# Polysketch attention and a multiplicative FFN on one core: 65 steps of the early program written in another order

## The chip, the cores and the metric

The kernel runs on one core of a Trainium2 chip. The core has five engines that each work through their own list of instructions in order: TensorE (PE in the profile; its weight loads are PEld), VectorE (DVE), ScalarE (ACT), GpSimd (POOL) and SyncE (SP, which here only issues DMAs). An instruction that waits for another engine holds up everything behind it on its own list. The metric is the device time of one execution in microseconds (us); before the change it is 245.37 us, the median of three runs.

## The reference

Sixteen heads (4 batches of 4) of sequence 1088 and width 32 go through an attention that sketches keys and queries, and the result, 4352 tokens of 128, goes through a feed-forward net whose two first products are multiplied element by element:

```
a = einsum('rd,bhsd->bhsr', S1, x);  b = einsum('rd,bhsd->bhsr', S2, x)     # r = 8
phi(x) = (a outer b), flattened to 64
kv  = einsum('bhsf,bhsd->bhfd', phi(k), v);   z = sum over s of phi(k)
att = einsum('bhsf,bhfd->bhsd', phi(q), kv) / (einsum('bhsf,bhf->bhs', phi(q), z) + 1e-6)
x   = att as (4352, 128)
out = (((x @ w1) * (x @ w2)) @ w3) @ w_out                                # 128 -> 1024 -> 1024 -> 128
```

The float64 words of the inputs are loaded raw and turned to float32 on the chip.

## The kernel before, in words

The kernel is one long straight program. `make_steps` defines 1,179 named steps, each a closure that issues one to a few dozen instructions; the string `ORDER` lists the names, and the kernel calls the steps in that order. Each instruction is tied to the one ahead of it on its engine, so `ORDER` is the order of every engine's list. Nothing is rescheduled later. `SLOTS` names the buffer that the n-th tile of a kind gets (for the kind `b` a PSUM bank), `POOL`, `ACTS` and `CPV` name steps that run on GpSimd, ScalarE or VectorE in place of their default engine.

Names of steps: `k0` to `k3` are the four batches of keys, `q0`, `q1`, ... parts of the queries, `w0` to `w10` the weights' conversions, `g0.4a` and the like the FFN of a group of 512 tokens (`a` the product with w1, `c` its copy out of PSUM, `b` the product with w2, `m` the multiplication of both), `s.` the sketch matrices, `warm` idle matmuls on zeros. The steps that matter for what follows:

- For each batch of keys, `k*.lead` and `k*.rest` split k into a coarse and a fine part (tile `kk`), `k*.gram0` to `gram4` multiply them on TensorE into the Gram matrix (`ps_g`, L659): nine columns of tokens, four heads, two products, each issued as two weight loads and two matmuls, 288 instructions in all.
- `k*.Gm`, `Gt`, `Ga`, `Gb` split that matrix on VectorE (`G_g`, `G_t`, `G_a`, `G_b`), `k*.T0` and `T1` multiply it with the sketches (`ps_T`, L883 to L891), `k*.Ta` and `Tb` split the result (`T_p`, L898 to L904), `k*.N0` and `N1` make the matrices for the denominator (`ps_N`, L912) and `k*.Na`, `Nb` split those (`N_g`, `RC`). `k0.kv0` to `kv3` accumulate the sketched keys with v (`ps_kv`, L769).
- `s.R` (L355) replicates the sketches to all heads, `s.c` copies them to `Sc`, `s.blkh` and `s.blk` make `Rh` and `RS` from it on GpSimd. `q0.A0` (L1038) needs `Rh`.
- `q0.C0t` is a VectorE transpose of `ps_c` (L1050), `q1.Ct` another one (L1130). `q0.xc0`, `xc1` (L1274) and `q0.xT0`, `xT1` (L1291) make `xT`, the input of the first FFN group, whose first product is `g0.4a` (L1799). `q1.pt0` and `q1.pt1` (L1246) transpose `ph` of the next queries, `q1.x` (L1297) multiplies it with `kz`.
- `k2.lead0` is VectorE work of 1152 columns that `k2.rest0` on GpSimd and then `k2.gram0` wait for; `k2.ab` (L727) sketches the keys of batch 2.

```
    for name in ORDER.split():
        n = len(traced)
        steps.pop(name)()
        ...
    for ins in traced[seen:]:
        if ins.engine in chained:
            if ins.engine in last:
                tc.add_manual_dep(ins, last[ins.engine].name, behind, reason="order")
            last[ins.engine] = ins
```

Of the kernel before, what the change touches and what calls it, by code (L numbers as in the profile page):

```python
# [26 lines left out]

SLOTS = {
    "b": 
        "012345670214657210671306537457462512346127340273014526045721472352140327540542370673245716"  # L30
        "210605643174306437107523543106572361507514502371054643535436051532410354273245554744570504"
        "7734023146507073701426351241254057163771361764573436046273673572571236574127105",
    "k_g": "0101",
# [48 lines left out]
kr1.load k2.zero k1.tr1 k1.kT1 kr0.kp warm9 k0.N0 warm10 k0.Na warm11 k0.T1 k0.kv0 k0.Tc k0.Tb k0.N1 k0.Nb k0.Nh q1.rm
q0.al k0.Nf q0.phi0 q0.phi1 q0.A1 q0.smy w1.m1 k1.max q0.sty q0.shy k0.kv3 k0.kv1 k0.kv2 q0.sly s.KS k0.kvr kr1.tr
k0.kvm w1.m0 kr1.kT q0.p01 q1.C0 q1.C1 q0.C1 k0.kzt k2.loadr q0.pt0 q0.C1t q0.scy q0.p2 k0.kz q0.pt1 k0.kvc kr1.ab
k0.kqt q0.p12 q0.dn q0.de q0.rc w1.j0 q0.pc0 q0.pc1 q0.x0 k1.kT0 q0.x1 q0.xs0 q0.xs1 q0.xt0 w1.a0 q1.A0 k2.load
w0.load k1.lead0 q0.xc0 q0.xc1 k0.kq w1.a1 k2.max q0.xt1 k1.ab q0.xT0 q0.xT1 g0.4a q1.load g0.5a q1.sm w0.m1 q1.st
# [5 lines left out]
g0.1m k2.gram1 k2.gram2 q3.max k2.gram3 g0.0c k2.kT0 k1.Nb q1.xT k2.gram4 q3.l2 k2.ab q2.A0 q2.C0 q2.C1 q3.l1 k1.kp0
v1.zero w9.c k2.abt g1.5a g1.5c g1.1a q2.Ct g1.7a q2.At q3.rm q3.A0 k0.Nr q2.sm q3.C0 q3.C1 k2.Gm v1.loadr q2.st w2.m
q2.sh g1.1c g1.2a k1.kp1 g0.6m q3.Ct g1.0a g1.7b k3.load v1.load g1.5b q3.At k2.Gt k3.loadr w2.c k2.Ga g0.0b w9.j
q2.sl g1.7c w6.c g1.6a k1.kv0 q3.sm k2.Gb w5.load q2.sc q2.al g1.0c k2.Gc g1.7m q2.p01 q3.st k1.kv2 k1.kv3 q3.sh w9.m
k1.kv1 k2.T0 k1.kvr q3.sl q2.p2 k2.T1 q2.p12 q2.dn q2.de g1.4a q2.rc k3.max g0.3b g0.0m g1.1b kh3.load g1.4c k2.Ta
g1.2b q3.sc g1.2c w5.c k2.Tc k1.kvc k1.kqt k1.kq g0.3m q3.p01 g1.6c g1.3a g1.5m g1.3b q2.bs q2.phi0 q2.pT0 g1.2m g1.3c
q2.x q2.load k2.N0 k2.Tb k3.lead0 w9.a1 k2.N1 g1.4b q3.al q3.p2 q3.p12 q2.xT0 g2.5a k3.kT1 g2.5c g2.6a q3.dn q3.de
k2.Na g1.3m g2.4a g2.3a w5.m g2.4b g2.6c k3.rest0 g1.0b k2.Nr q3.rc g1.1m g1.4m g1.6b k2.Nb g0.2b kr1.kp w6.j q4.tr
g2.4c g1.6m w7.load w7.c q3.bs q4.max q2.restT w6.m w5.j w2.j q4.l2 w3.load w9.a0 k3.gram0 k3.gram1 k3.gram2 q3.load  # L100
w7.j q3.phi0 k3.gram3 k3.gram4 g2.2a k3.Gc g2.1a g1.0m w2.a0 g2.6b g2.0a g2.4m g2.1c f6.t w6.a0 w4.load g2.3b w2.a1
g2.2b g2.2c g2.0c w6.a1 g2.1b q3.pT0 k3.Gm g0.2m k3.Gt k3.kT0 v3.load w7.m f6.m w5.a1 w5.a0 g2.3c k3.Ga k3.Gb g2.3m
w7.a0 g2.1m w3.m g2.6m q3.x k3.T0 k3.T1 f2.t w3.c w3.j w8.load g2.0b q3.xT0 g3.1a f6.o k3.Ta g3.0a g3.0b g2.7a g2.7b
q4.l1 w7.a1 q4.rm g3.0c g3.0m g2.5b v3.loadr g3.3a w4.c g2.0m g2.2m g3.1c g2.5m g2.7c g2.7m v2.zero g3.6a k3.Tb
v2.loadr k3.ab f4.t k3.Tc k3.abt w4.j g3.3c w3.a1 q4.A0 q4.C0 q4.C1 q4.At k3.N0 k3.N1 v2.load w3.a0 f0.t k2.kp1 f4.m
w4.m g3.6c q3.restT q6.tr g3.6b g3.6m q4.Ct q4.sm w10.load f0.m k2.kp0 f4.o g3.1b f0.o g3.1m qr.max q6.max k3.kp1
q4.st k2.kv0 w4.a1 k3.kp0 k2.kv3 k2.kv1 k2.kv2 k2.kvr q4.sh qr.l2 k3.kv0 k3.kv1 f3.t k2.kvc k3.kv3 k3.kv2 k3.Na w4.a0
qr.l1 qr.rm q4.sl q4.sc q4.al k3.kvr k3.kvc g3.4a q6.l2 g3.4c g3.4b q4.p01 k3.Nr g3.3b q6.l1 w8.c g3.5a k3.Nb g2.4o
g3.4m f1.t f3.m w10.c k3.kqt g3.5c w8.m g3.3m q4.p2 q6.rm k3.kq f1.m f1.o q6.A0 q6.C0 w10.j q6.C1 g3.1o f3.o w8.j
q4.p12 q6.At g3.2b w10.m q6.Ct q4.dn g3.7a q6.sm q6.st w8.a0 w10.a0 qr.A0 qr.C0 qr.C1 g3.0o g2.1o g3.7c w10.a1 g0.3o  # L110
qr.Ct qr.At q6.sh q4.de g1.4o q4.rc q4.bs g3.5b q4.na w8.a1 f2.m f2.o q6.sl q6.sc g2.3o f7.t qr.sm g3.5m q4.nb q4.nm
g3.2a qr.st g3.2c g1.6o q4.nr q4.ne q4.nn q4.phi0 g0.2o q6.al k2.kqt f5.t g3.2m f5.m f5.o q4.phi1 q4.pT0 g3.7b g3.7m
qr.sh g3.6o f7.m k2.kq g0.4o q4.pT1 f7.o v.s v.t q4.x q4.xT2 q6.p01 g3.4o q6.p2 g2.7o g1.2o q6.p12 qr.sl g0.6o q6.dn
q6.de g1.5o q4.xT0 qr.sc qr.al q6.rc q6.bs q4.xT1 q6.nb q6.na q6.nm q6.nr q6.ne v.1 q6.nn q6.phi0 q4.xT3 q6.phi1 o.S3
q6.pT0 h4.s1 q6.pT1 g0.1o g0.0o g0.5o g0.7o g1.0o h4.s2 g3.5o g0.oT g1.7o q6.x g1.1o g2.5o qr.p01 qr.p2 qr.p12 qr.dn
g3.3o qr.de qr.rc qr.bs qr.phi0 qr.pT0 g3.2o q6.xT0 q6.xT1 q6.xT2 o.S1 g2.2o v.2 g3.7o q6.xT3 qr.x qr.xT0 g1.3o g2.0o
# [33 lines left out]
def make_steps(ctx, tc, q, k, v, S1, S2, moe_w1, moe_w2, moe_w3, moe_w_out, out):  # L150
    nc = tc.nc
    dve, act, pe, pool, sp = nc.vector, nc.scalar, nc.tensor, nc.gpsimd, nc.sync
    B, H, S, D = q.shape
# [689 lines left out]
    def k_end(b):  # L843
        a = acc[b]
        tag = "t"

# [63 lines left out]
        def by_head(o, P, x, start, stop):  # L910
            for h in range(H):
                pe.matmul(o[h * D:(h + 1) * D], P, a["Tp"][:, x, h], start=start, stop=stop,  # L912
                          tile_position=(0, h * D), skip_group_check=True)
# [1021 lines left out]
```

## Time and profile before

| what | value |
|---|---|
| runs | 245.28 to 245.43 us, median 245.37 us |
| span of the profiled execution, first to last instruction | 244.1 us |
| what lies around the span (median less span; the profiled execution has no time of its own besides) | 1.27 us |
| TensorE clock granted, mean | 0.998 |
| busy: PE / DVE / ACT / POOL | 97% / 85% / 51% / 66% of the span |
| PE instructions shown | 2724 matmuls and 2724 weight loads |
| DMA | 22.06 MB, most of it in the first 100 us |
| instructions fetched by DMA during the span | queue q8: 21 transfers, 0.34 MB; queue q14: 10 transfers, 0.08 MB |

The share of busy time is a mean over stages. TensorE is counted busy for nearly the whole span, but in the first microseconds part of that is the idle matmuls on zeros. "issue" as the cause of a wait means that the engine waited for nothing that the profile shows.

### The profile page before, as it was taken

What the parts mean: (1) busy time and instruction counts of PE and PEld (TensorE: products, weight loads), DVE (VectorE), ACT (ScalarE), POOL (GpSimd) and SP (SyncE); (2) the same over time, 40 slices, a digit from 0 to 9 for tenths busy, and PEclk for the clock granted to TensorE, in tenths of its full rate; (3) what the DMA queues carried; (4) which work ended last, traced back from release to release, by engine and by line L of the source; (5) the groups of instructions that cost most, each with busy time, mean ns of one, the idle gap of its engine ahead of it and who ended that gap; (6) DMA issues with size and microseconds to landing.
All of it is one profiled execution on the core that took longest, in us unless ns stands there. A gap on an engine that the chain in (4) does not pass through costs nothing.

```text
span 244.1 us, 6745 instructions
## 1 busy us (share of the span) xinstructions
PE 236.2 (97%) x2724; PEld 129.8 (53%) x2724; DVE 206.7 (85%) x421; ACT 123.5 (51%) x246; POOL 161.9 (66%) x203
## 2 busy tenths in 40 slices
...
GB/s 201 265 143 325 181 227 190 6 197 224 220 141 251 188 217 190 59 1 3 3 0 0 4 0 3 59 113 3 1 0 0 0 3 0 0 1 3 12 90 93
DMA packets 31935, 22.06 MB, mean 90 GB/s; under 512 B 21280, under 2 KB 26528, under 8 KB 31904
## 3 DMA queue, kind: packets, MB, share of 16 engines
...
q8 instruction: 21, 0.34, 0.6%
...
q14 instruction: 10, 0.08, 0.1%
...
## 4 chain that ended last, share of the span: by engine, by line
PE 87%; DMA 5%; ACT 2%; POOL 2%; DVE 1%; issue 1%; POOLq 0%; SPq 0%
PE b_ps L1809 12%; PE ps_o L1835 12%; PE ps_X L1673 11%; PE a_ps L1799 11%; PE ps_o L1759 10%; PE ps_w3o L534 6%; PE ps_Y L1673 6%; PE ps_Z L1673 3%; PE ps_g L659 2%; PE ps_x L1527 2%; PE ps_ac L1374 2%; DMA qh<-in_q_dram 2%; DMA k<-in_k_dram 2%; PE ps_or L1824 2%; POOL ph L1208 1%; PE idle_ps L255 1%
## 5 line engine op out<-in xcount | busy, mean ns | idle before, releaser
L1673 PE MATMUL ps_X<-xd,wv 64*128 64x512 f32 x112 | 36.3, 593 | 0.0
L1799 PE MATMUL a_ps<-xT,w 128*128 128x512 f32 (+1 forms) x80 | 36.1, 562 | 0.0
L1809 PE MATMUL b_ps<-xT,w 128*128 128x512 f32 (+1 forms) x80 | 35.6, 555 | 0.0
L1804 ACT COPY ffa<-a_ps 128x512 f32<-128x512 f32 (+1 forms) x38 | 20.1, 540 | 29.2 <-PE a_ps L1799 26.7
L1707 POOL TENSOR_TENSOR hc<-hc 128x512 f32<-128x512 f32 x16 | 20.7, 1304 | 15.7 <-DVE hc L1685 15.5
L1835 PE MATMUL ps_o<-ab,w3o 128*128 128x512 f32 x64 | 29.6, 600 | 0.0
L1680 ACT COPY hc<-ps_X 128x512 f32<-128x512 f32 x38 | 21.3, 590 | 16.1 <-PE ps_X L1673 12.9
L1815 DVE TENSOR_TENSOR ab<-ffa,b_ps 128x512 f32<-128x512 f32 (+1 forms) x40 | 23.9, 623 | 4.9 <-PE b_ps L1809 4.1
L501 POOL TENSOR_TENSOR w3c<-w3c,cv_m 128x512 int32<-128x512 int32 x16 | 21.2, 1344 | 4.2 <-DVE w3c L495 4.1
L1673 PEld LDWEIGHTS ps_X<-xd,wv 64*128 64x128 f32 x112 | 14.9, 186 | 13.1 <-issue 10.9
L1799 PEld LDWEIGHTS a_ps<-xT,w 128*128 128x128 f32 x80 | 14.1, 189 | 13.9 <-issue 8.8
L1809 PEld LDWEIGHTS b_ps<-xT,w 128*128 128x128 f32 x80 | 14.4, 190 | 13.1 <-issue 8.1
L1673 PE MATMUL ps_Y<-xd,wv 64*128 64x512 f32 x48 | 19.7, 594 | 0.0
L1835 PEld LDWEIGHTS ps_o<-ab,w3o 128*128 128x128 f32 x64 | 11.6, 190 | 13.4 <-issue 13.0
L534 PEld LDWEIGHTS ps_w3o<-wo,w3T 128*128 128x128 f32 x128 | 15.3, 192 | 2.4 <-issue 2.4
L534 PE MATMUL ps_w3o<-wo,w3T 128*128 128x128 f32 x128 | 15.7, 276 | 0.0
L1759 PE MATMUL ps_o<-hc,w3o 128*64 128x512 f32 x32 | 15.1, 595 | 0.0
L1759 PE MATMUL ps_o<-tt,ws 128*64 128x512 f32 x32 | 13.7, 594 | 0.0
L1680 ACT COPY hc<-ps_Y 128x512 f32<-128x512 f32 x14 | 8.1, 592 | 9.7 <-PE ps_Y L1673 6.6
L263 ACT ACTIVATE cv_c<-raw 128x1024 f32<-128x1024 f32 (+1 forms) x13 | 13.0, 1014 | 0.0
L1540 ACT COPY xd<-ps_x 64x256 f32<-64x256 f32 x24 | 8.8, 367 | 7.2 <-PE ps_o L1835 6.8
...
## 6 DMA issues: line engine op xcount, KB each, us to landing
...
```

The costliest lines, as they stand in the source:

```text
L263: act.activation(dst, hi.bitcast(F32), ACT.Prelu, scale=2.0 ** -112, alpha=-2.0 ** 32)
L501: pool.tensor_tensor(d, d, x["m"][:, i * 512:(i + 1) * 512], ALU.add)
L534: pe.matmul(t["o"], w3T[ko][:, c], wo[:, c], start=c == 0, stop=c == NC - 1)
L1673: pe.matmul(x[bank], stat(j, u)[:, i * 128:(i + 1) * 128], rows(j, u), start=new, stop=True, tile_position=(u * 64, 0), skip_group_check=True)
L1680: cp(n(y))(x[k], x[bank])
L1707: on(f"h{g}.{i}m{k}").tensor_mul(both[0][k], both[0][k], both[1][k])
L1759: pe.matmul(acc_o[bank][half[0]:half[1]], w(i), x(i), start=n == 1, stop=n == (2 if j == 3 else 4), tile_position=(0, half[0]), skip_group ...
L1799: pe.matmul(x["a"][:, :w], w_of(0, c), xT[g][:, c0:c0 + w], start=True, stop=True)
L1804: cp(f"g{g}.{c}{su}c")(x["s"][:, :w], x["a"][:, :w])
L1809: pe.matmul(x["b"][:, :w], w_of(1, c), xT[g][:, c0:c0 + w], start=True, stop=True)
L1815: dve.tensor_mul(ab_sb[g, c][:, c0:c0 + w], x["s"][:, :w], x["b"][:, :w])
L1835: pe.matmul(o_ps[g], w3o[:, c], ab_sb[g, c], start=n == 1, stop=n == NC)
```

## The change

65 steps stand elsewhere in `ORDER`, all between the 30th and the 345th name. No step is added or removed, and none runs on another engine. (`CPV` loses three names of steps whose branch for batches 2 and 3 never asks `CPV`.) `SLOTS` is rewritten where the order in which tiles are made has changed, so that every tile shares its buffer with the same tiles as before; only two of the idle matmuls' results go to another PSUM bank. Two short edits let `T0` and `N0` keep a tile that exists already; they issue the same instructions. Lines of the kernel are one less than before up to the edit at `T0`, one more behind that, three more behind the edit at `N0`.

```diff
 CPV = set("""
-    g0.0c g0.1c h4.1ac h4.1ad h6.1bc h6.2ad k0.kT1 k1.kvc k2.kT1 k2.kq k3.kT0 k3.kT1 k3.kq q0.xc0
-    q0.xc1 q6.xT0 q6.xT2
+    g0.0c g0.1c h4.1ac h4.1ad h6.1bc h6.2ad k0.kT1 k1.kvc k2.kq k3.kq q0.xc0 q0.xc1 q6.xT0 q6.xT2
 """.split())
...
-warm3 s.rest w1.load s.T s.P s.tc warm4 q0.l2 k0.kT1 s.Pc s.R k0.g k0.lead0 s.c s.blk k0.rest0 q1.tr k0.gram0 s.blkh
-k1.zero s.Pm warm5 q0.l1 q0.A0 warm6 kr0.ab k0.lead1 q0.rm q0.sma q0.sta warm7 k0.kT0 v0.load v0.loadr k1.load k0.ab1
+warm3 s.rest w1.load s.T q0.l2 s.tc s.P s.Pc k0.kT1 k0.g k0.lead0 k0.rest0 k0.gram0 s.R warm4 q1.tr k1.zero q0.l1 s.c
+s.blkh s.Pm warm5 s.blk q0.A0 warm6 kr0.ab k0.kT0 q0.sma k0.lead1 q0.sta warm7 q0.rm v0.load v0.loadr k1.load k0.ab1
...
         @step(f"k{b}.T0")
         def _():
-            a["T"], a["Tr"] = two([D, H, r], "ps_T")
+            a["T"], rest = two([D, H, r], "ps_T")
+            if rest is not None:
+                a["Tr"] = rest
...
         @step(f"k{b}.N0")
         def _():
-            a["N"], a["Nq"] = two([128, r], "ps_N")
+            a["N"], rest = two([128, r], "ps_N")
+            if rest is not None:
+                a["Nq"] = rest
```

So `s.R` and the idle matmuls of `warm4` now stand behind `k0.gram0` on TensorE, and both `k0.ab` groups stand ahead of `k0.gram1` to `gram4`, with `q0.C0` behind them. Three places in the order of the engines follow.

VectorE, around the Gram matrix of batch 0, before (`s_bs<-ps_c` is `q0.C0t`, the rows with `T_` are `k0.Ta`, `kp` is `k0.kp0`, `N_g` begins `k0.Na`):

```order
L651 TENSOR_TENSOR kk<-k,kk 128x4x160
L1050 STREAM_TRANSPOSE s_bs<-ps_c 128x256
L1097 TENSOR_TENSOR s_hla<-ps_a,s_hla 128x128
L217 TENSOR_REDUCE G_g<-ps_g 128x1
L201 SCALAR_TENSOR_TENSOR G_t<-G_g,ps_g 128x32
L204 SCALAR_TENSOR_TENSOR G_a<-G_g,G_t 128x32
L865 TENSOR_TENSOR G_b<-ps_g,G_a 128x32
L466 TENSOR_SCALAR w_81<-cv_c 128x2x256
L898 TENSOR_REDUCE T_g<-ps_T 32x4
```

The same place after the change:

```order
L203 SCALAR_TENSOR_TENSOR s_hla<-s_ga,s_t 128x128
L1100 TENSOR_TENSOR s_hla<-ps_a,s_hla 128x128
L216 TENSOR_REDUCE G_g<-ps_g 128x1
L200 SCALAR_TENSOR_TENSOR G_t<-G_g,ps_g 128x32
L203 SCALAR_TENSOR_TENSOR G_a<-G_g,G_t 128x32
L1053 STREAM_TRANSPOSE s_bs<-ps_c 128x256
L864 TENSOR_TENSOR G_b<-ps_g,G_a 128x32
L465 TENSOR_SCALAR w_81<-cv_c 128x2x256
L899 TENSOR_REDUCE T_g<-ps_T 32x4
```

The transpose of `ps_c` moved from ahead of the Gram matrix's split into the middle of it, ahead of `T_g`.

VectorE, where the first FFN group's input is made, before:

```order
L1198 RECIPROCAL s_rc<-s_rc 128x16
L466 TENSOR_SCALAR w_81<-cv_c 128x2x256
L1274 COPY xc<-ps_xt 128x256 x2
L1291 TENSOR_TENSOR xT<-xc,ps_xs 128x256 x2
L1137 TENSOR_REDUCE s_g<-ps_a 128x32
L201 SCALAR_TENSOR_TENSOR s_t_699<-s_g,ps_a 128x256
L1130 STREAM_TRANSPOSE ay_C<-ps_c 128x384
```

After:

```order
L1201 RECIPROCAL s_rc<-s_rc 128x16
L465 TENSOR_SCALAR w_81<-cv_c 128x2x256
L1277 COPY xc<-ps_xt 128x256 x2
L1133 STREAM_TRANSPOSE ay_C<-ps_c 128x384
L1294 TENSOR_TENSOR xT<-xc,ps_xs 128x256 x2
L1140 TENSOR_REDUCE s_g<-ps_a 128x32
L200 SCALAR_TENSOR_TENSOR s_t_701<-s_g,ps_a 128x256
```

The transpose `ay_C<-ps_c` moved ahead of the two operations that write `xT`. On ScalarE a copy of `k1`'s transposed keys (`k1.kT0`, L690) moved ahead of the two copies of `pT` that `q0.x0` and `x1` read, a little earlier in the program.

TensorE, from the transposes of `q1` to the Gram matrix of batch 2, before:

```order
L1246 MATMUL ps_ph<-ident,ph 128x128 x4
L1799 MATMUL a_ps<-xT,w_81 128x512 x2
L1809 MATMUL b_ps<-xT,w_81 128x512
L1246 MATMUL ps_ph<-ident,ph 128x128 x4
L1809 MATMUL b_ps<-xT,w_81 128x512
L912 MATMUL ps_N<-T_p,P2a 32x8 x4
L912 MATMUL ps_N<-T_p,P2b 32x8 x4
L912 MATMUL ps_N<-T_p,P2s 32x8 x8
L1297 MATMUL ps_x<-pT,kz_605 64x512 x2
L659 MATMUL ps_g<-kk 32x64
L659 MATMUL ps_g<-k,kk 32x32
```

After:

```order
L1802 MATMUL a_ps<-xT,w_81 128x512
L1249 MATMUL ps_ph<-ident,ph 128x128 x4
L1802 MATMUL a_ps<-xT,w_81 128x512
L1812 MATMUL b_ps<-xT,w_81 128x512
L913 MATMUL ps_N<-T_p,P2a 32x8 x4
L913 MATMUL ps_N<-T_p,P2b 32x8 x4
L913 MATMUL ps_N<-T_p,P2s 32x8 x8
L1249 MATMUL ps_ph<-ident,ph 128x128 x4
L1802 MATMUL a_ps<-xT,w_81 128x512
L1812 MATMUL b_ps<-xT,w_81 128x512
L658 MATMUL ps_g<-kk 32x64
L658 MATMUL ps_g<-k,kk 32x32
```

`k1.N0` and `N1` moved ahead of the second transpose, a product each with w1 and w2 now stands directly ahead of the Gram matrix, and `q1.x` is no longer there. It stands inside the Gram matrix of batch 2, behind `gram3`, 256 instructions after the matrix's first:

```order
L658 MATMUL ps_g<-kk 32x64
L658 MATMUL ps_g<-k,kk 32x32
L1300 MATMUL ps_x<-pT,kz_605 64x512 x2
L658 MATMUL ps_g<-kk 32x64
L658 MATMUL ps_g<-k,kk 32x32
```

On VectorE `k2.lead0` moved ahead of `k1.Ta` there, and on TensorE `k1.T1` ahead of a product with w1.

More of the change, by code (lines that the diff above doesn't have):

```diff
@@ L29 @@
     "b":
[L30 removed]
+        "012345670412657210763106753574462512346127340273014526045721752431240327540542370673245716"
         "210605643174306437107523543106572361507514502371054643535436051532410354273245554744570504"
@@ L82 @@
[L82 to L86, printed above, removed]
@@ L87 @@
-q1.Ct g0.4c g0.4b q1.sh q1.sl k1.rest0 g0.7b w0.c1 g0.7a k1.abt w0.j1 k1.gram0 w0.c0 s.RC q1.scy k1.gram1 kh2.load
-q1.sca q2.tr g0.5c q1.al q1.p01 q1.p2 k1.gram2 k1.gram3 kr1.abc k1.gram4 w6.load w0.m0 g0.6b w0.j0 g0.7c g0.7m k1.Gm
-q1.p12 k1.Gc g0.0a w2.load w0.a1 q1.dn q1.de q1.rc q1.bs k1.Gt g0.3a k1.Ga k1.T0 k2.kT1 k1.Gb g0.3c q1.restT g0.2a
-q1.phi k1.T1 q1.pt0 g0.4m w0.a0 q2.max q2.l2 g0.6a k1.Ta k2.lead0 k2.rest0 g0.1a g0.2c k1.Tc g0.5b q3.tr g0.5m k1.Tb
-q1.pc0 q1.pt1 g0.1b w9.load k1.N0 s.AR q2.l1 q2.rm v3.zero q1.pc1 k1.N1 q1.x g0.6c g0.1c k1.Na k1.Nr k3.zero k2.gram0
@@ L92 @@
[L92 to L116, printed above, removed]
@@ new lines @@
+k0.ab0 k0.rest1 q0.sha k0.gram1 k0.gram2 k0.gram3 k0.gram4 q0.C0 k0.abc1 q1.max q0.sla q1.l2 k1.loadr w1.c1 k0.Gm
+k0.Gt s.Pp k0.Ga q0.C0t k0.Gb k0.abc0 q1.l1 warm8 k0.T0 kr0.abc k0.kp1 q0.sca w1.j1 k0.Ta k0.kp0 k0.Gc w1.c0 k2.zero
+k1.tr0 kr1.load k1.tr1 k1.kT1 warm10 warm9 k0.N0 k0.Na k0.T1 k0.kv0 warm11 k0.Tc q0.al k0.Tb k0.N1 kr0.kp k0.Nb k0.Nh
+q1.rm k0.Nf q0.phi0 q0.A1 q0.phi1 q0.smy w1.m1 k1.max q0.sty q0.shy kr1.tr k0.kv3 k0.kv1 q0.sly s.KS k0.kv2 k0.kvr
+k0.kvm w1.m0 kr1.kT q0.p01 q1.C0 q1.C1 q0.C1 k0.kzt k2.loadr q0.pt0 q0.C1t q0.scy q0.p2 k0.kz q0.pt1 k0.kvc q0.p12
@@ new lines @@
+kr1.ab k0.kqt q0.dn q0.de q0.rc k1.kT0 q0.pc0 w1.j0 q0.x0 q0.pc1 q0.x1 q0.xs0 q0.xs1 q0.xt0 w1.a0 q1.A0 k2.load
+k1.lead0 w0.load q0.xc0 q0.xc1 k0.kq w1.a1 k2.max q0.xt1 q1.Ct q0.xT0 q0.xT1 k1.ab g0.4a g0.5a w0.m1 q1.sm q1.load
+q1.st g0.4c g0.4b q1.sh q1.sl k1.rest0 g0.7b w0.c1 k1.abt g0.7a k1.gram0 w0.c0 w0.j1 s.RC q1.scy k1.gram1 kh2.load
+q1.sca q2.tr g0.5c q1.al q1.p01 q1.p2 k1.gram2 k1.gram3 kr1.abc k1.gram4 w6.load w0.m0 g0.6b w0.j0 g0.7c g0.7m k1.Gm
+q1.p12 g0.0a k1.Gc w2.load w0.a1 q1.dn q1.de q1.rc k1.Gt q1.bs g0.3a k1.Ga k1.T0 k1.Gb k2.kT1 g0.3c q1.restT k1.T1
@@ new lines @@
+q1.phi g0.2a g0.4m q1.pt0 w0.a0 q2.max q2.l2 k2.lead0 g0.6a k1.Ta k2.rest0 q3.tr g0.2c k1.Tc g0.5b k1.Tb g0.5m q1.pc0
+k1.N0 k1.N1 q1.pt1 g0.1a w9.load g0.1b k1.Na q2.l1 s.AR v3.zero q1.pc1 q2.rm g0.6c g0.1c k3.zero k1.Nr k2.gram0 g0.1m
+k2.kT0 k2.gram1 k2.gram2 q3.max k2.gram3 g0.0c q1.x k1.Nb q1.xT q3.l2 k2.gram4 k2.ab q2.A0 q2.C0 q2.C1 q3.l1 k1.kp0
+v1.zero w9.c k2.abt g1.5a g1.5c g1.1a q2.Ct q2.At g1.7a q3.rm q3.A0 k0.Nr q2.sm q3.C0 q3.C1 k2.Gm v1.loadr q2.st q2.sh
+g1.1c w2.m g1.2a k1.kp1 g0.6m q3.Ct g1.0a g1.7b k3.load v1.load g1.5b q3.At k2.Gt k3.loadr w2.c g0.0b w9.j k2.Ga q2.sl
```

32 lines of the change are left out of this document (26 added, 6 removed).

## The prediction

> **What bounds the kernel now.** First the page's busy times and the chain that ended last, then TensorE's own waits in the first 62 us.
>
> ```profile
> PE 236.2 (97%) x2724; PEld 129.8 (53%) x2724; DVE 206.7 (85%) x421; ACT 123.5 (51%) x246; POOL 161.9 (66%) x203
> PE 87%; DMA 5%; ACT 2%; POOL 2%; DVE 1%; issue 1%; POOLq 0%; SPq 0%
> ```
>
> ```profile
> PE ps_g L659 <- issue: 1.6, 2, 1.2
> PE ps_kv L769 <- issue: 0.9, 1, 0.9
> ...
> PE ps_ph L1246 <- POOL ph L1208: 0.2, 1, 0.2
> ```
>
> TensorE carries 87% of the chain and does the same matmuls after the change, so the time moves by TensorE's idle time and by whatever makes it late ahead of its dense part. Of its idle time 2.5 us, in three waits, have no engine behind them, and they stand in runs of very short matmuls. How far apart they are shows what they are. The windows go from the end of the first wait to the start of the second, from the end of the second to the start of the third, and from the end of the third to 147.82 us (busy us and count of PE, PEld, DVE, ACT and POOL, then clock, DMA share, GB/s):
>
> ```profile
> 14.27:19.44 5.17, 5.17 (x124) 4.25 (x125) 3.88 (x16) 3.70 (x10) 3.21 (x7) 1.00 0.51 153
> 20.35:45.83 25.48, 24.90 (x505) 14.51 (x505) 21.46 (x57) 18.72 (x40) 15.59 (x19) 1.00 0.73 191
> 46.98:147.82 100.84, 100.83 (x1395) 57.77 (x1395) 91.05 (x189) 53.00 (x97) 70.00 (x62) 1.00 0.41 103
> ```
>
> 124 + 125 are 249 instructions, 505 + 505 are 1010. The view leaves out semaphore instructions; the built program has 7 and 14 of them in these stretches, which makes 256 and 1024, four times 256. So TensorE's program comes in pieces of 256 instructions (the page's 21 transfers on q8, 16 KB each), and it waits where a piece isn't there. The DMA view of the 0.1 us from 44.2, and then of that from 147.8, holds one transfer of such a piece each:
>
> ```profile
> q8 instruction: 1, 0.02, 71.8%
> q8 instruction: 1, 0.02, 57.4%
> ```
>
> 71.8% of 16 engines for 0.1 us are 1.15 us of transfer, landed at 45.4; TensorE went on at 46.98. The piece before it was entered 256 instructions ahead of the wait, at the end of `ps_N` at 43.1 (chain below): 3.9 us from entry to use. The other transfer, by the third window, starts when 2 x 1395 + 15 semaphores = 2805 instructions have run, 11 short of 11 x 256: ahead of a row of slow matmuls the fetch runs ahead of execution, by 11 instructions and those of the start-up, at most 44.2 - 43.1 = 1.1 us or 5 instructions at 0.43 us per pair. I take 16.
>
> [...]
>
> **The change, part by part.** *Gram matrix of batch 0.* Chain and VectorE rows:
>
> ```profile
> 9.18 0.35 PE ps_s L355 x2
> 9.52 0.57 PE ps_g L659 x22
> 10.63 0.09 PE ps_a L1038 x4
> 11.23 0.84 PE ps_ab L702 x8
> 12.07 0.79 PE ps_c L1030 x24
> 12.87 1.00 PE ps_g L659 x48
> 13.86 0.41 issue
> 14.27 0.58 PE ps_g L659 x23
> ...
> 8.66 0.69 DVE L651 TENSOR_TENSOR kk<-k,kk 128x512 f32<-128x512 f32 x1
> 12.93 0.45 DVE L1050 STREAM_TRANSPOSE s_bs<-ps_c 128x256 f32<-128x256 f32 x1
> 15.59 0.19 DVE L865 TENSOR_TENSOR G_b<-ps_g,G_a 128x32 f32<-128x32 f32 x1
> 16.10 0.18 DVE L898 TENSOR_REDUCE T_g<-ps_T 32x4 f32<-32x32 f32 x1
> 18.27 0.17 DVE L904 TENSOR_TENSOR T_p<-ps_T,T_p 32x32 f32<-32x32 f32 x1
> 20.35 0.69 PE L769 MATMUL ps_kv<-kp,v 128*32 128x64 f32 x34 [0.91 <-issue]
> ```
>
> `gram0` cannot start before `rest0` ends at 9.35, so `s.R` behind it ends at 9.45 + 0.57 + 0.35 = 10.4 where it ended at 9.5. Through `Sc` and `Rh`, `A0` (10.63) slips 0.85, to 11.5. From its end to `gram1` took 2.14 us; with the second `ab` (0.84) in place of `ps_c` (0.79) it starts at 13.7. 1.00 + 0.58 us of matmuls end at 15.3, against 14.85: the 0.41 wait is gone, since the piece was usable at 14.27 and its first instruction now comes up at 15.1, 25 ahead of the matrix's end. `ps_c` then ends at 16.1, and the transpose that reads it has moved ahead of `G_b` and `T_g`: `G_b` 16.1 + 0.4 = 16.5 in place of 15.59, so `T_g`, `kp` and the later `T_p` come 0.9 later; `N1`, which needs that `T_p`, ends at 19.85 (18.93). The third piece's first instruction is now the 26th of `kv1` and comes up at 20.25. When is it there? Entered at 15.0, it is by the same piece's row (14.27 to 20.35, 6.1 us) there at 21.1, and by the piece at 43 us (3.9) at 18.9. The rest of `kv`, 0.8 us, then ends at 21.9 or at 21.05; before, what follows it began at 21.4. So TensorE goes on 0.5 later or 0.3 earlier. What decides is 5.2 us, half-way between the two rows, and neither is nearer: I take +0.1 and keep both ends.
>
> *First FFN input.*
>
> ```profile
> 24.83 0.61 ACT L690 COPY kT<-ps_kt 128x512 f32<-128x512 f32 x1
> 25.71 0.74 DVE L1274 COPY xc<-ps_xt 128x256 f32<-128x256 f32 x2
> 26.48 0.79 DVE L1291 TENSOR_TENSOR xT<-xc,ps_xs 128x256 f32<-128x256 f32 x2
> 27.98 0.57 DVE L1130 STREAM_TRANSPOSE ay_C<-ps_c 128x384 f32<-128x384 f32 x1
> 27.42 1.96 PE L1799 MATMUL a_ps<-xT,w 128*128 128x512 f32 x4
> ```
>
> The transpose of 0.57 goes ahead of `xT`, whose end at 27.27 lets the FFN begin, and the copy `kT` delays `xc` by about 0.4. The transpose fills part of no other wait, so `xT` ends 0.4 later (0.3 to 0.6; a gain is excluded, since VectorE has no idle time here to give). From there TensorE works without a gap to 38.13, where it waits 0.24 for `ph`. Both terms reach that place as 0.1 + 0.4 - 0.24 = +0.26; with the ends of the first, -0.1 and +0.66.
>
> *Gram matrix of batch 2.* The chain before, and VectorE's waits around it:
>
> ```profile
> 41.60 0.44 PE ps_ph L1246 x4
> 42.03 0.86 PE b_ps L1809 x2
> 42.90 0.36 PE ps_N L912 x32
> 43.26 1.01 PE ps_x L1297 x4
> 44.27 1.56 PE ps_g L659 x75
> 45.83 1.16 issue
> 46.98 0.54 PE ps_g L659 x15
> ...
> 38.16 0.18 DVE L898 TENSOR_REDUCE T_g<-ps_T 32x4 f32<-32x32 f32 x1 [0.34 <-PE ps_T L891]
> 41.63 0.69 DVE L1815 TENSOR_TENSOR ab<-ffa,b_ps 128x512 f32<-128x512 f32 x1 [0.64 <-PE b_ps L1809]
> 48.21 0.78 DVE L745 STREAM_TRANSPOSE kabt<-ps_ab 128x256 f32<-128x256 f32 x2 [0.18 <-PE ps_ab L727]
> ```
>
> In the built program the piece boundary now falls on the matrix's first instruction, the next on `q1.x`. The 16 instructions ahead of the first boundary are the products `b` and `a` and the transposes: with run-ahead the piece behind it is asked for at their start, 0.44 + 0.86 + 0.86 us ahead of the matrix, and 256 of its instructions take 1.6: 3.8 us against 3.9, a wait of 0.1 in place of 1.16. The matmuls behind the old wait ran slow (0.54 for a sixth of the matrix); undisturbed they take 0.3. That is -1.3 for TensorE. VectorE must follow: its idle time up to 48.21 is 0.34 + 0.64 + 0.18 = 1.16, and the change fills the first (with `k2.lead0`) and moves `b` ahead of the second. So -1.1, between -1.16 and, without any run-ahead, a wait of 3.9 - 1.6 = 2.3 in place of 1.16: +1.1.
>
> *The rest* costs nothing: the step pairs swapped on ScalarE, GpSimd and VectorE between 50 and 57 us only trade places within work whose consumer, TensorE, runs without a gap there. SP's DMAs keep their order; the load behind `v1.zero` starts when TensorE is through batch 2's matrix, so it moves with it.
>
> Sum: 244.1 + 1.27 around it (the median 245.37 less the span; the profiled execution itself is given no other time) + 0.26 - 1.1 = 244.5 us.
>
> **Rivals.** (1) The waits are a stall of dense matmuls, not of pieces, and 1.16 us stays in the matrix: 245.37 + 0.26 = 245.6. For it: all three stand in dense runs. Against it: the distances of 256, and the third window, which holds runs as dense (`ps_kv`, `ps_ac`) and has TensorE busy for 100.83 of its 100.84 us. [...] (2) The third piece is late by its own row, 6.1 us: 245.37 + 0.66 - 1.1 = 244.95. (3) The fetch doesn't run ahead here, for the transposes at its start wait for nothing and are short: the matrix waits 2.3 us and 245.37 + 0.26 + 1.1 = 246.7. It decides from a lead under 1.15 us, where the matrix waits as long as before. (4) TensorE comes 0.8 us earlier out of 48 us, and the weights' conversions on GpSimd, busy 9.86 of 10 us from 80 to 90, are no earlier: the gain turns into a wait there, 245.4.
>
> ```profile
> 80.00:90.00 10.00, 10.00 (x105) 5.88 (x104) 9.78 (x16) 7.60 (x13) 9.86 (x9) 1.00 0.87 206
> ```
>
> **How the numbers follow.** Forecast and the case of the piece in time 50% (243.9 to 244.8 by the ends of the first two terms), rival (2) 20%, (1) 7%, (4) 10%, (3) 13%. A measurement tells about 0.2% (0.49 us) from no change. Faster than 244.88: the forecast and a third of (2), 56%. Slower than 245.86: (3), 13%. Within: 31%. The range 243.9 to 245.8 leaves out (3) and a little of the fast end.
>
> **What would show it.** No "issue" wait in batch 0's matrix; `T_g` 0.9 later; `A0` at 11.5; a wait in `ps_kv` of 0 to 0.9; `a_ps` starting at 27.4 to 28.3; in batch 2's matrix a wait under 0.4 and `ps_ab` at 46.7 to 47.4. It is wrong if that wait is over 1 us, if `a_ps` starts past 28.5, or if TensorE idles after 50 us.

## The result, and the profile after

| | before | after |
|---|---|---|
| median of six runs each, alternating on one chip | 245.43 us | 247.15 us |
| ratio after / before, 95% interval | | 1.0068 (1.0051 to 1.0085) |
| span of the profiled execution | 244.1 us | 245.4 us |
| its own time | none given | 247.24 us |

Here and below a time is the median of all executions, while a ratio leaves out the slow ones (607 and 247.96 us of the kernel before, 704 us of late_x_shift18).

The change costs 1.7 us; 244.5 us was forecast. TensorE's waits in the changed kernel (waiting line, what it waited for, us, times, longest):

```profile
PE ps_g L658 <- issue: 1.6, 1, 1.6
...
PE ps_T L884 <- DVE G_a L203: 0.7, 1, 0.7
PE a_ps L1802 <- DVE xT L1294: 0.4, 1, 0.4
PE ps_xt L1270 <- ACT pT L1237: 0.3, 1, 0.3
PE ps_kv L768 <- DVE kp L676: 0.3, 1, 0.3
```

Of the three "issue" waits before, the two in batch 0 are gone. The third, in batch 2's matrix, has grown from 1.16 to 1.6 us, and new short waits for VectorE and ScalarE have come. The chain through batch 2's matrix (start, us, what):

```profile
42.39 0.86 PE a_ps L1802 x2
43.25 0.86 PE b_ps L1812 x2
44.11 1.61 PE ps_g L658 x79
45.72 1.59 issue
47.31 0.19 PE ps_g L658
47.50 1.01 PE ps_x L1300 x4
48.51 0.33 PE ps_g L658 x15
48.84 0.59 PE ps_ab L726 x16
```

The matrix starts at 44.11 (44.27 before), but the product `ps_x`, which ran ahead of it before, now lies behind its wait: TensorE does nothing from 45.72 to 47.31, then comes `ps_x`. `ps_ab` starts at 48.84 in place of 47.53, 1.31 later, and that is the 1.3 by which the span has grown: from 50 to 200 us TensorE is busy without a gap in both kernels. The 1.31 are two parts: the wait ends 0.33 later (47.31, before 46.98), and from there to `ps_ab` it is 1.53 us in place of 0.55, for `ps_x` still stands there.

The piece that TensorE waits for starts its transfer at 45.07; the DMA view of the 0.1 us from 45.0 holds it:

```profile
q8 instruction: 1, 0.02, 54.8%
```

Batch 0, first the chain, then VectorE, then GpSimd (start, us, engine, line, operation):

```profile
10.27 0.33 PE ps_s L354 x2
...
11.58 0.10 PE ps_a L1041 x4
```

```profile
12.93 0.83 DVE L650 TENSOR_TENSOR kk<-k,kk 128x640 f32<-128x640 f32 x1
13.67 2.26 DVE L203 SCALAR_TENSOR_TENSOR s_hla<-s_ga,s_t 128x128 f32<-128x128 f32 x1
15.97 0.29 DVE L1100 TENSOR_TENSOR s_hla<-ps_a,s_hla 128x128 f32<-128x128 f32 x1
16.17 0.18 DVE L216 TENSOR_REDUCE G_g<-ps_g 128x1 f32<-128x32 f32 x1
...
17.49 0.17 DVE L899 TENSOR_REDUCE T_g<-ps_T 32x4 f32<-32x32 f32 x1
```

```profile
13.83 1.95 POOL L676 TENSOR_TENSOR kp<-kab 128x1024 f32<-128x1024 f32 x1
```

`s_hla` of 128 columns took 2.26 us and ended at 15.93, 0.15 after GpSimd's `kp` ended at 15.78. The matrix was complete at 15.4, yet `G_g` begins only at 16.17 and `T_g` at 17.49 (16.10 before). The first FFN product starts at 28.25 (27.42), behind `xT`:

```profile
28.25 1.96 PE L1802 MATMUL a_ps<-xT,w 128*128 128x512 f32 x4 [0.41 <-DVE xT L1294]
```

### The profile page after: what moved, and what is told of

Read it like the earlier page. It is cut to its first block, busy times and chain, and to the rows that moved or that the text cites. A ratio compares the mean times of both kernels' runs of the same rounds, so it can differ in the third digit from the quotient of the medians.

```text
span 245.4 us, 6743 instructions
## 1 busy us (share of the span) xinstructions
PE 237.0 (97%) x2724; PEld 130.3 (53%) x2724; DVE 211.0 (86%) x421; ACT 123.9 (50%) x246; POOL 163.7 (67%) x203
## 4 chain that ended last, share of the span: by engine, by line
PE 85%; DVE 7%; DMA 4%; issue 2%; POOL 1%; ACT 1%; ACTq 0%; DVEq 0%
PE ps_o L1838 12%; PE b_ps L1812 11%; PE ps_X L1676 11%; PE a_ps L1802 11%; PE ps_o L1762 10%; PE ps_w3o L533 6%; PE ps_Y L1676 6%; PE idle_ps L254 3%; PE ps_Z L1676 3%; PE ps_x L1530 2%; PE ps_ac L1377 2%; DMA raw<-in_moe_w_dram 2%; PE ps_g L658 2%; PE ps_or L1827 2%; DMA raw<-in_moe_w_out_dram 2%
## 5 line engine op out<-in xcount | busy, mean ns | idle before, releaser
L1710 POOL TENSOR_TENSOR hc<-hc 128x512 f32<-128x512 f32 x16 | 20.7, 1305 | 15.8 <-DVE hc L1688 15.7
L1683 ACT COPY hc<-ps_X 128x512 f32<-128x512 f32 x38 | 21.3, 590 | 16.1 <-PE ps_X L1676 12.9
L1676 PEld LDWEIGHTS ps_X<-xd,wv 64*128 64x128 f32 x112 | 14.9, 186 | 13.2 <-issue 10.6
```

The costliest lines, as they stand in the source:

```text
L1676: pe.matmul(x[bank], stat(j, u)[:, i * 128:(i + 1) * 128], rows(j, u), start=new, stop=True, tile_position=(u * 64, 0), skip_group_check=True)
L1683: cp(n(y))(x[k], x[bank])
L1710: on(f"h{g}.{i}m{k}").tensor_mul(both[0][k], both[0][k], both[1][k])
```

## The experiments

Seventeen kernels ran in five groups, each on one chip with the kernel before beside it: before_again, late_only, early_only and shift32; x_earlier, before_x_late, early_sha and before_shift78; the two mix and two late_x kernels; the three hold kernels; the two swap kernels. The kernel before had medians of 245.21, 245.21, 245.52, 245.32 and 245.69 us there, so ratios compare better across groups than times.

**The kernel before once more.**

> The kernel before, unchanged, for its span beside its time and for how far its waits vary from one execution to the next. Theory A (pieces of the program): the same three waits of TensorE at the same three instructions, 0.4, 0.9 and 1.2 us within 0.3 each, time 245.4. The second question is what lies around the span: the changed kernel shows 1.8 us in all its runs; if the kernel before shows 1.8 too (span about 243.6 at a time of 245.4), the execution profiled before was one of the longer ones and 0.5 us of the prediction's miss is its base; if it shows 1.3, the change itself lengthens what lies outside the span.

245.41 us, ratio 1.0024 (0.9999 to 1.0049) to itself: differences under 0.25% are not told apart here. Of theory A's three waits two came within its 0.3 (0.17 and 1.16), the one of 0.9 did not. The profiled execution has a span of 243.4 us at 245.2, so 1.8 us lie around the span, as in all runs of the changed kernel. The kernel before that the prediction read was an execution 0.7 us longer in its span, and the reason stands in TensorE's row for the sketch of `k` and `v`: it had a wait of 0.91 there, in this execution none is listed, and the only wait left in batch 0 is

```profile
14.34 0.22 PE L659 MATMUL ps_g<-k,kk 128*32 128x32 f32 x1 [0.17 <-issue]
```

So the 0.9 us wait that the change removes is there in some executions only.

**One half of the moves at a time.**

```diff
 late_only:  ORDER = names 1 to 188 as before, 189 to 1179 as after
 early_only: ORDER = names 1 to 136 as after, 137 to 1179 as before
```

> Only the moves from the 189th name on (Gram matrices of batches 1 and 2 and what follows) are made; everything ahead is in the old order. The piece boundary then falls two slow FFN matmuls ahead of batch 2's matrix, and ahead of the semaphore wait that stands in front of it, in place of on its first instruction. Theory A (the wait in batch 2's matrix is a piece asked for too late, and the semaphore in front held the asking): asked for about 0.9 us earlier, the wait falls from 1.6 to 0.4-0.8 us; with the old order ahead, no loss there; 244.6 to 245.0 us. Theory B (the new order around batch 2 itself makes the wait, wherever the boundary stands): the wait stays 1.5 or more, 245.8 to 246.0 us.

> Only the moves up to the 135th name (batch 0: sketches, Gram matrix, kv) are made; the rest in the old order. Theory A: TensorE's waits of 0.4 and 0.9 us in batch 0 go, but VectorE's s_hla waits 2 us for GpSimd's kp, T_g comes 1.3 later, N1 1.7 later, and TensorE starts the products behind kv 0.4 later than before; the wait in batch 2's matrix is as before, 1.2 (its boundary shifts by 2 instructions); 245.7 to 245.9 us. Theory B (the early part is neutral or a gain, all of the loss is late): 245.0 to 245.4 us.

| kernel | us | ratio (95%) |
|---|---|---|
| late_only | 246.95 | 1.0072 (1.0047 to 1.0097) |
| early_only | 246.03 | 1.0030 (1.0013 to 1.0048) |

Both halves lose. In late_only theory A is refuted, and the time lies 0.9 us above theory B's as well: the boundary lies in the last FFN product ahead of the matrix, ahead of the semaphore instruction, and the wait is as long as in the changed kernel:

```profile
45.42 1.63 issue
```

early_only came somewhat above its theory A (246.03 for 245.7 to 245.9) and far from B. In late_only four of eleven executions (247.42 to 248.77 us) have a mean granted clock of 0.991 to 0.993, the others 0.997 or more. The two losses add up to more than the whole change (0.72 + 0.30 against 0.68%), so one may hide part of the other; by the widths of the intervals this is not certain.

**Moving the piece boundaries, order untouched.** In shift32 the first 27 idle matmuls are cut into 43 narrower ones, so that the boundaries of TensorE's 256-instruction pieces fall 32 instructions earlier in the work; before_shift78 does the same to the kernel before, by 78.

```diff
-WARM = [27, 2, 3, 4, 4, 4, 1, 2, 1, 1, 2, 2]
+WARM = [43, 2, 3, 4, 4, 4, 1, 2, 1, 1, 2, 2]   # shift32: the first 43 with 160 columns
+WARM = [54, 2, 3, 8, 8, 8, 1, 2, 1, 1, 2, 2]   # before_shift78: those of 8 and 54 with 128 columns
```

> The changed kernel with its order untouched, but the first 27 idle matmuls of 256 columns are 43 of 160 columns, as many columns in all: 32 more instructions on TensorE ahead of everything, so that each piece boundary falls 32 instructions earlier in the work. The boundary on batch 2's first matrix instruction falls into the ps_N products at 41.5 us, the next one 225 instructions into the matrix. Theory A (pieces): asked for 2.4 us earlier the piece is there in time, the wait of 1.6 us falls under 0.3, and 1.2 to 1.6 us go: 245.5 to 246.0 us. Theory B (the wait belongs to the place: dense matmuls, the semaphore, or x behind the matrix): it stays at 1.6 ahead of x, 247.1 us.

> The kernel before, its order untouched, with 39 of its early idle matmuls split in two (128 columns each in place of 256): 78 more instructions on TensorE, so that each piece boundary falls 78 instructions earlier in the work. Theory A (pieces): the fetch behind batch 2's wait is asked for at 40.6 us in place of 43.1; even if it waits 3 us for the weights' load it is there at 46.2 or before, when the boundary, 78 instructions earlier, comes up at 45.3: a wait of 0 to 0.9 in place of 1.2-1.4. Both waits in batch 0 move 78 instructions earlier and shrink to 0-0.5 each, 244.0 to 245.0 us. Theory B (the waits belong to their places): nothing changes, 245.2 to 245.5 us.

shift32: 247.2 us, 1.0084 (1.0058 to 1.0110). The wait moved by exactly those 32 instructions, from in front of `x` to in front of the last 32 of the matrix's instructions ahead of `x` (14 matmul rows are shown there, one in the changed kernel):

```profile
45.34 1.47 issue
46.81 0.41 PE ps_g L659 x14
```

That it goes with the count of instructions, and not with the place, shows that it is the piece that is missing. All traces agree: counted through TensorE's rows (matmuls, weight loads, semaphore and drain instructions), the row that ends such a wait has 1729 rows ahead of it in batch 2's matrix, in each of the 18 traces that have the wait, and 449, 705 or 961 in batch 0 and at 22 us, all in steps of 256. But the wait didn't shrink and the time is theory B's, so theory A's "asked for in time" is wrong: the piece that covers `ps_N` at 41.4 was entered 3 us ahead of the transfer of the next, which started at 44.39.

before_shift78: 250.6 us, 1.0232 (1.0184 to 1.0279); both theories failed. The wait in batch 2's matrix is gone, as A said, but a new one has come at 22 us, in the products `ps_cy`, which no row of the kernel before would have named:

```profile
PE ps_cy L1031 <- issue: 3.1, 1, 3.1
```

There a piece was entered at 18.9 us, the transfer of the next started 4.0 later, under data loads (DMA share 1.03 in between, so all engines busy), and the piece ran out after 3.3 us.

**One product inside the piece or behind it.**

```diff
 x_earlier, from the kernel after; before_x_late is the reverse, from the kernel before
-k2.gram1 k2.gram2 q3.max k2.gram3 g0.0c q1.x
+k2.gram1 q1.x k2.gram2 q3.max k2.gram3 g0.0c
```

> The changed kernel with one step moved: the product q1.x (1.08 us of TensorE, 8 instructions) stands between the second and the third part of batch 2's matrix, in place of between the fourth and the fifth. So it lies inside the 256 instructions that run while the next piece is fetched, not behind them. Theory A (wait = time from entering a piece until the next one can be used, 3.4 us with the DMA engines idle, less the run time of the 256 instructions): these take 2.8 us in place of 1.8, the wait falls from 1.6 to 0.4-0.7 us, 246.0 to 246.4 us. Theory B (the wait belongs to the matrix's dense matmuls, wherever x stands): 1.6 us, 247.1 us.

> The kernel before with the same single step moved the other way: q1.x behind the fourth part of batch 2's matrix, as in the changed kernel, in place of ahead of the matrix. Theory A: the 256 instructions behind the boundary lose x and take 1.8 us in place of 2.5-2.8, the wait grows from 1.2-1.4 to 1.7-1.9 us; 245.7 to 246.1 us against 245.3. Theory B (x's place doesn't matter, the rest of the late moves costs the time): 245.2 to 245.5 us.

x_earlier: 245.84 us, 1.0020 (1.0004 to 1.0037), 1.2 us less than the change by the ratios. The product of 1.01 us runs while the piece is fetched, and the wait is 0.44:

```profile
44.86 1.01 PE ps_x L1300 x4
45.87 0.86 PE ps_g L658 x43
46.73 0.44 issue
47.17 0.54 PE ps_g L658 x16
```

before_x_late: 247.1 us, 1.0071 (1.0049 to 1.0093), 1.0 to 1.4 above theory A. Five of its ten executions have a mean granted clock of 0.990 to 0.993 and take 246.95 to 248.78 us; of the other five, at 0.997 or more, four take 246.06 to 246.71 and one 248.23. The profiled one, the longest, shows what happens with the clock:

```profile
45.22 2.05 issue
47.27 0.22 PE ps_g L659 x2
47.49 1.84 PE ps_x L1297 x4
```

```profile
48.50:49.50 1.00, 1.00 (x12) 0.24 (x14) 0.00 (x0) 0.12 (x1) 0.00 (x0) 0.50 0.00 0
```

Behind the wait of 2.05 us TensorE's granted clock is 0.50 (third number from the end) until about 51 us, and `ps_x` takes 1.84 us for 1.01. So a single step, moved, costs as much as the whole change (0.71 against 0.68%), but not in the same way: the four take 246.3 us on average, about 1 us over the kernel before, and the rest comes with the long executions, most of them at a lower clock, which no theory had. The changed kernel's own six executions have clocks of 0.998 to 1.0.

**Putting `s_hla` back.**

```diff
 early_sha, from early_only
-q0.sta warm7 q0.rm v0.load v0.loadr k1.load k0.ab1 k0.ab0 k0.rest1 q0.sha
+q0.sta q0.sha warm7 q0.rm v0.load v0.loadr k1.load k0.ab1 k0.ab0 k0.rest1
```

> The early moves alone (as in early_only, 246.0 us) with one VectorE step put back ahead of two: q0.sha (s_hla) right behind q0.sta, ahead of q0.rm and k0.rest1, so that it runs before GpSimd begins kp. Theory A (the early part loses because s_hla, 0.3 us elsewhere, takes 2.3 us while GpSimd's kp runs, and holds the split of batch 0's matrix): s_hla 0.3 us, G_g 0.5 earlier, T_g 0.3 to 0.5 earlier, 245.5 to 245.8 us. Theory B (the early loss is ahead of it: s.R behind gram0, A0 0.9 later, and the later steps wait for that anyway): 245.9 to 246.1 us.

245.39 us, 1.0004 (0.9984 to 1.0025), 0.64 us less than early_only by the medians; theory A, a little better than it said. VectorE in early_sha:

```profile
12.14 0.29 DVE L204 SCALAR_TENSOR_TENSOR s_hla<-s_ga,s_t 128x128 f32<-128x128 f32 x1
...
15.23 0.19 DVE L217 TENSOR_REDUCE G_g<-ps_g 128x1 f32<-128x32 f32 x1 [1.16 <-PE ps_g L659]
...
16.67 0.17 DVE L898 TENSOR_REDUCE T_g<-ps_T 32x4 f32<-32x32 f32 x1
```

and in early_only:

```profile
13.39 2.25 DVE L204 SCALAR_TENSOR_TENSOR s_hla<-s_ga,s_t 128x128 f32<-128x128 f32 x1
...
17.20 0.17 DVE L898 TENSOR_REDUCE T_g<-ps_T 32x4 f32<-32x32 f32 x1
```

Ahead of `kp` the step takes 0.29 us and beside `kp` 2.25, and in early_sha `kp` itself takes 2.38 us in place of 1.95, begun while VectorE's `kk<-k,kk` runs. Not every VectorE step pays: in the kernel before, `kp` ran from 12.87 to 14.81, and beside it the transpose `s_bs<-ps_c` took 0.45 us and `s_hla<-ps_a,s_hla` 0.25, where the changed kernel, behind `kp`, has 0.44 and 0.29. The one recorded first isn't spared: in the changed kernel `s_hla` is recorded from 13.67 and `kp` from 13.83, and it is `s_hla` that waits. That the company of `kp` costs the time is measured; why, no run shows.

**Both repairs, and the transpose in front of `xT`.**

```diff
 mix_new_mid    = after, with the moves of x_earlier and early_sha
 mix_old_mid    = mix_new_mid, names 137 to 188 as before (q1.Ct behind q0.xT1, k1.kT0 behind q0.pc1)
 late_x_earlier = late_only, with the move of x_earlier
 late_x_shift18 = late_x_earlier, with the first 27 idle matmuls as 36 of 192 columns
```

> The changed kernel with both repairs: q1.x between the second and third part of batch 2's matrix, and s_hla back ahead of q0.rm and k0.rest1. Theory A (two separate losses that add): 245.84 (x_earlier) less the 0.64 that the s_hla repair gave to the early moves alone, 245.1 to 245.5 us. Theory B (the same TensorE waits absorb both, only the longer counts): 245.7 to 245.9 us.

> As mix_new_mid, but the names from the 137th to the 188th in the old order: the transpose q1.Ct behind xT, k1.kT0 behind the copies pT. Theory A (the transpose ahead of xT costs TensorE 0.4 us at the start of the first FFN product, as the prediction had it): 0.3 to 0.45 us under mix_new_mid, 244.7 to 245.1 us. Theory B (the later wait for ph takes it back, the prediction's 0.24): 0.0 to 0.2 us under it.

> The old order up to the 188th name, the new one behind it with q1.x between the second and third part of batch 2's matrix (late_only with that one move). Theory A: late_only's wait of 1.9 us falls to 0.5-0.9, and with it the long executions; 244.8 to 245.2 us, against 246.95 for late_only. Theory B (the late moves lose elsewhere too): 245.5 us or more.

> As late_x_earlier, with the first 27 idle matmuls of 256 columns as 36 of 192: 18 more instructions, so that the boundary in front of batch 2's matrix falls behind ps_N at about 41.1 us, ahead of the semaphore wait, the transposes and the last b product. Theory A: the fetch is asked for at 41.1; the weights' load ends at 42.9 in the old early order, so it starts by 43.1 at the latest and is usable by 45.7; the next boundary comes up at 46.2: no wait, 0.4 to 0.9 us under late_x_earlier, 244.1 to 244.6 us. Theory B (the load holds it until 44.4 as in shift32): usable at 46.8, a wait of 0.6 as in late_x_earlier, no difference.

| kernel | us | ratio (95%) |
|---|---|---|
| mix_new_mid | 245.49 | 0.9990 (0.9968 to 1.0012) |
| mix_old_mid | 245.58 | 1.0006 (0.9989 to 1.0023) |
| late_x_earlier | 245.38 | 0.9992 (0.9971 to 1.0014) |
| late_x_shift18 | 245.31 | 1.0000 (0.9977 to 1.0023) |

The two repairs together bring the change back to the kernel before, as theory A of mix_new_mid said; no version is clearly ahead of it. late_x_earlier ends 1.57 us under late_only by one move (0.8% by the ratios), within 0.2 of theory A and short of B; its wait is 0.71, late_only's was 1.63 and not 1.9, and none of its executions has a clock under 0.997. The transpose ahead of `xT` costs nothing that shows; mix_old_mid is not under mix_new_mid, as B nearly said, and not 0.3 to 0.45 under it: in mix_new_mid TensorE waits for `xT`, in mix_old_mid for `ph` as long (one row of each):

```profile
PE a_ps L1802 <- DVE xT L1294: 0.4, 1, 0.4
```

```profile
PE ps_ph L1249 <- POOL ph L1211: 0.4, 1, 0.4
```

late_x_shift18 went as its theory B: entered at 41.76, transferred from 44.88, a wait of 0.80 (the 1.0 in its profile is batch 0's).

**What holds back the fetch: the load?** Both shifted kernels had a weights' load on the DMA engines, until about 44 us in shift32 and 44.5 in late_x_shift18. The next three kernels take it away: `w9.load` ahead of `w2.load`, and the first DMA of the latter waits for the first part of batch 2's matrix.

```diff
+        if name == "w2.load":          # now behind k2.gram0 in ORDER
+            first = [i for i in traced[n:] if i.engine == nc.sync.engine][0]
+            ahead = [i for i in traced[:n] if i.engine == nc.tensor.engine][-1]
+            tc.add_manual_dep(first, ahead.name, landed, reason="hold")
```

> shift32 (247.2 us, the fetch entered at 41.4 and started at 44.4) with the weights' loads taken out of the way: w9.load goes ahead of w2.load, and w2.load's first DMA waits for the first part of batch 2's matrix, so that the DMA engines are idle from about 41 to 44 us. Theory A (the transfer of a piece stands behind the data loads): it starts 0.7-1.2 us after entry, at 42.1-42.6, is usable by 45.3, and the wait of 1.5 us falls under 0.3; 245.5 to 246.0 us if w2's later arrival costs nothing. Theory B (a fetch starts only at a certain place of the program or fill of a buffer): it still starts at 44.4, wait 1.5, 247.2 us.

> The changed kernel with the loads moved in the same way and nothing else. The boundary is the matrix's first instruction, entered at 43.5 at the earliest, behind the semaphore wait. Theory A: the fetch starts at 44.3-45.0 whether the DMA engines are idle or not, a wait of 1.2 to 1.6, 246.7 to 247.2 us: idle DMA engines alone don't help. Theory B (the load alone was the cause): the wait falls under 0.5, 246.0 us.

> late_x_shift18 (245.3 us, a wait of 1.0 in batch 2's matrix, its fetch entered at 41.8 and started at 44.9 behind the load) with the loads moved in the same way. Theory A: the fetch starts at 42.5-43.0, usable by 45.6, the boundary comes up at 46.7: no wait, 244.2 to 244.8 us, under the kernel before. Theory B: no change, 245.3 us; or w2's load comes too late for its conversion and TensorE waits for weights behind 50 us, 245.5 us or more.

248.3 us, 1.0114 (1.0066 to 1.0162); 247.04 us, 1.0069 (1.0045 to 1.0092); 245.26 us, 1.0006 (0.9973 to 1.0038). Theory A's reason fell. In hold_shift32 the DMA engines moved nothing at all from 40.8 to 44.8 us (last two numbers), the piece was entered at 41.7, and the transfer still started within the 0.1 us from 44.8:

```profile
40.80:44.80 4.00, 4.00 (x92) 2.02 (x94) 3.53 (x10) 2.72 (x6) 3.21 (x4) 1.00 0.00 0
```

```profile
q8 instruction: 1, 0.02, 59.1%
```

```profile
45.70 1.47 issue
```

hold_only went as A said (transfer at 44.67, a wait of 1.35). So the load is not the cause in this place. hold_late_x_shift18 gained nothing (transfer at 44.96), as its theory B said. hold_shift32 lies 1.1 us above its theory B, and its profile has waits for loads that shift32 has not (`ps_krt` 0.7 us for `kr`), so its time says little.

That a load can hold a fetch back shows at the piece behind, which these kernels enter under the load that they moved: its transfer starts 2.36, 3.67 and 2.94 us (in the order above) after TensorE enters the piece ahead of it, in the other 16 traces 0.7 to 1.2 us (DMA share 0.99 from 47.0 to 50.8 us in hold_only, 0.08 from 47.3 to 48.4 in the changed kernel). In hold_late_x_shift18 this makes a new wait of 0.5 us in `ps_ac`.

**The semaphore in front of the matrix?** In 18 of the 19 traces, all but before_shift78, the transfer started 1.05 to 1.53 us after the semaphore instruction that stands in front of batch 2's matrix and waits for its PSUM bank (in the changed kernel it passes at 43.54, ScalarE's copy `ffa<-a_ps` ends at 43.50). In the changed kernel and in swap_only, where the matrix takes a bank that is free earlier, that instruction stands at (from and to, us):

```profile
L658 PEldq EVENT_SEMAPHORE  x1: 51/51/51, 43.5 to 43.5; - x1
```

```profile
L658 PEldq EVENT_SEMAPHORE  x1: 51/51/51, 43.1 to 43.1; - x1
```

```diff
 swap_only: in SLOTS, banks 1 and 2 exchanged from k2.gram0 on (k2.gram0 2 for 1, q1.x 1 for 2, ...)
 swap_shift32: the same, with the idle matmuls of shift32
```

> shift32 with two PSUM banks exchanged from batch 2's matrix on: the matrix takes the bank that ScalarE has read by 41.1 us, and q1.x the one that it reads until 43.5. So the semaphore instruction in front of the matrix, which passed at 43.3 to 43.7 in every run so far, can pass at about 42.2, when TensorE's list comes to it. In 12 of 13 traces the transfer of the piece started 1.05 to 1.53 us after that instruction, wherever the boundary lay and whether the DMA engines were idle. Theory A (the list stands still at that instruction, and the fetch is asked for behind it): the transfer starts at 43.2 to 43.6 in place of 44.4, the wait of 1.5 us falls to 0.2-0.6, 246.0 to 246.4 us. Theory B (the two only coincide; the request waits for the matrix itself, whose operand kk is there at 43.07): it starts at 44.1 to 44.4, the wait stays 1.2 to 1.5, 246.8 to 247.2 us.

> The changed kernel with the same exchange of banks and no shift: the boundary is the first instruction of the matrix, right behind the semaphore instruction. Theory A: that passes at 42.2, the transfer starts at 43.3 to 43.7 in place of 45.07, the wait of 1.6 us falls to 0.2-0.6, 245.8 to 246.2 us. Theory B: as it is, the wait stays 1.3 to 1.6, 246.7 to 247.2 us.

246.84 us, 1.0050 (1.0017 to 1.0082), and 246.75 us, 1.0068 (1.0034 to 1.0102): the times are theory B's and don't tell the two from the changed kernel (two of swap_only's ten executions, at 249.1, have a clock of 0.990; the others take 246.18 to 247.17). The traces do, in part. The instruction passed 0.4 to 0.5 us earlier (42.82 and 43.14; TensorE's list gets there no sooner; without the exchange it passes at 42.4 to 43.8 in the 16 traces beside before_shift78) and the transfer started with it, 1.16 and 1.23 us behind, at 43.98 (44.39 in shift32) and 44.37 (45.07 after). In swap_only the wait is

```profile
45.81 0.86 issue
```

in place of 1.59, though the matrix itself began 0.09 later than in the changed kernel; in swap_shift32 it is 1.25 in place of 1.47. Neither fell to A's 0.2 to 0.6, but the start follows that instruction and not the matrix, as A says; with a shift of half a microsecond in two kernels this is likely, not shown. Why the transfer waits for it although the piece was entered 2.0 us before that (shift32), and why in before_shift78 it started 3.4 us ahead of it, stays open. One count fits all 19 traces: in the 18 the semaphore instruction stands at most 32 rows behind the one that enters the piece (256 rows ahead of the one that ends the wait). In before_shift78 it stands 80 rows behind; the semaphore instruction ahead of it, 15 rows in front of the piece, passes at 41.15, and the transfer starts 1.35 us after that one, like the others. A request that goes out when TensorE's list has come some 33 to 79 rows into the piece would do this; no run tests it.

## Why the prediction was wrong, by its own steps

- **Gram matrix of batch 2: the step that failed.** "With run-ahead the piece behind it is asked for at their start", 16 instructions ahead, hence a wait of 0.1 and -1.1 us. The 16 came from one row at 147.8 us, among matmuls that wait for nothing. Here the semaphore instruction in front of the matrix passes only 0.5 us ahead of it (43.54 against 44.04; 1.0 before), and the transfer started at 45.07. The wait was 1.59, so this term is +0.43 us in the profile, not -1.1. (The rest of the miss lies ahead: the place where `x` began at 43.26 is now reached at 44.11, +0.85 where +0.26 was taken.) That is rival (3), 246.7 us at 13%, in its time; its reason, short transposes, was not the one, and its price, 2.3, was too large, since from the first instruction at 44.04 to the end of the wait at 47.31 it was 3.3 us, not 3.9 (the old piece was entered in a different place). That it came near the measured 247.15 is in part luck, for it has neither the +0.85 nor the place of `x`. What the step missed altogether is which slow work lies in the 256 instructions: the product of 1.01 us was inside before and behind the boundary after, and x_earlier shows that moving it back inside is worth 1.2 us.
- **Gram matrix of batch 0: right in its moves, wrong in one size.** `s.R` ended at 10.6 (10.4 forecast), `A0` was at 11.58 (11.5), there is no "issue" wait in the matrix, `ps_c` ended at 16.1 (16.1). But `T_g` came 1.39 later, not 0.9, for VectorE's `s_hla` stood behind GpSimd's `kp`, and no term had a price for a VectorE step that is held up by a GpSimd one. `N1` ended at 20.7 (19.85), and what follows `kv` began at 21.79 in place of 21.40: +0.39 where +0.1 was taken, inside the range given. Against the second trace of the kernel before, which has no wait in `kv` (20.64), it is 1.15. Rival (2) didn't come: the piece was in time.
- **First FFN input: right in the trace, too small to show in the time.** `a_ps` started at 28.25, inside 27.4 to 28.3, with the wait of 0.4; the wait for `ph` went, as said. mix_new_mid against mix_old_mid bounds the net at about +-0.3 us; the +0.16 that was taken (0.4 less 0.24) lies inside.
- **The base.** 1.27 us around the span was the median less the span of another execution; it is 1.8 in every run, and the execution that was read was 0.5 us longer than the median. Nothing in one trace tells that, but a range could have held it.
- **The rest costs nothing, no idle TensorE behind 50 us:** right. Rival (4) had nothing to give back, and rival (1) fell with shift32: the waits are pieces. Behind 20 of the 21 transfers in the changed kernel no "issue" wait is listed; the one in batch 2's matrix has its wait of 1.59 us on the path, and one move takes 1.2 us off the time.
